# A mixture-of-experts tail: one more expert's last wide slot and remainder share a pair of tiles, and the short slots change places

## The chip, the core and the metric

The kernel runs on one core of a Trainium2 chip. The metric is device time in microseconds of one execution; what is compared is the median of several executions of each kernel. One further execution was taken by the hardware profiler; its rows are what the prediction reads.

## The reference, cut to what matters

```python
# attention, 8 batches of 2496 tokens, 256 features, z has 64
scores = (1 / S) * z @ z.T
out = u * ((maximum(scores, 0) ** 2) @ v)          # x: 19968 tokens of 256

# mixture of 8 experts, one per token
e_idx = argmax(x @ w_gate, axis=1)
for e in range(8):
    mask = e_idx == e
    h = maximum(x[mask] @ w1[e], 0)                # 256 -> 1024
    out[mask] = gate_w * sigmoid(...) * (h @ w2[e]) # 1024 -> 256
```

With the inputs of this case the experts get 2334, 2603, 2530, 2412, 2622, 1984, 2769 and 2714 tokens. Modulo 512 that leaves remainders of 286, 43, 482, 364, 62, 448, 209 and 154.

## The kernel before, in words

The first half of the time is attention. While it runs, each finished chunk of tokens is gated and scattered by GpSimd (POOL) into a list in DRAM, `xs`, that is sorted by expert. The second half, which starts near 1312 us of the span, is the mixture: a fixed list of *slots*, each with a fixed number of places n for tokens of one expert. What a slot's expert and first row are comes from small tables that the kernel computes while it runs (`full_table`, `rest_table`), so the list's shape is the same whatever the counts are.

One slot does this, in an order written out by hand in `run`:

- SyncE (SP) loads the tokens (`load_x`) and the expert's weights, 8 tiles of 256 KB (`load_w`). A slot issues these for the slot two further on. A weight load that has no `always` is skipped when the same buffers hold that expert already.
- ScalarE (ACT) and VectorE (DVE) split each weight tile into a high and a low part (`split_w`, L842 and L843), one tile at a time between the steps of the slot before; they also turn and split the next slot's tokens (`turn`, `split_x`).
- `up`: TensorE (PE) computes 1024 hidden features, 6 matmuls of n columns for each 128 of them (L897), 48 in all. The bank in PSUM is then read by ACT, which writes `hh` (L906), and by DVE, which writes `hl` (L907).
- `down`: PE multiplies back to 256 features. There are two ways. *By columns* (L976): 48 matmuls of n columns; then DVE turns the result (L986), multiplies it by the token's factor (L989), and POOL writes it out with one indirect DMA for every 32 tokens (L993), so 16 of them for 512 places and 10 for 320. *By rows* (L936): 24 matmuls of 256 columns for every 128 tokens; ACT applies the factor (L944) and POOL writes with one indirect DMA for every 128 tokens (L950). Slots of 128, 256 and 384 places go by rows, the others by columns.

The slots: 27 wide ones of 512 places (three of them by rows), and then the list that the change is about. There each expert's remainder gets a slot, and the experts are ranked by the size of the remainder. In the kernel before, the six largest have a slot of their own of 512, 448, 384, 320, 256 and 256 places, and the two smallest (62 and 43 here) are taken together with their expert's last whole 512 in a *pair* of slots that share one set of weights: 320 + 320 and 320 + 256 places. Six wide slots are left beside them. In the text the wide ones are W0 to W5, the remainders R512, R448, R384, R320, R256 and R256b, and the pairs P1a + P1b (320 + 320) and P2a + P2b (320 + 256). The order is

```
W0 R512 W1 R448 W2 R384 W3 R320 W4 R256 W5 P1a P1b P2a P2b R256b
```

The four wide ones W2 to W5 belong to one expert; W3, W4 and W5 skip their weight load. A second list (`more_slots`) behind a branch takes what does not fit; it has nothing to do with these inputs.

Of the kernel before, what the change touches and what calls it, by code (L numbers as in the profile page):

```python
# [7 lines left out]
F32 = mybir.dt.float32  # L8
F32R = mybir.dt.float32r
BF16 = mybir.dt.bfloat16  # L10
I32 = mybir.dt.int32
# [6 lines left out]
P = 128  # L18
B, S, D, DQ = 8, 2496, 256, 64
N = B * S  # L20
E, F = 8, 1024
# [3 lines left out]
TW = 512  # L25
# [2 lines left out]

N_FIRST = -(-(N - S - E * (TW - 1)) // TW)
N_MAX = N // TW - N_FIRST  # L30
N_FULL = N_MAX - E // 2 - 2

SIZES = (512, 448, 384, 320, 256, 256)

PAIRS = ((320, 320), (320, 256))

RESTS = tuple((k, 0, n) for k, n in enumerate(SIZES))
RESTS += tuple((k, at, n) for k, ab in enumerate(PAIRS, len(SIZES)) for at, n in zip((0, ab[0]), ab))
BEYOND = ((1, 384, 128), (2, 384, 128), (3, 256, 256), (4, 256, 256), (5, 256, 256), (6, 640, 384), (7, 576, 448))
ROOM = SIZES + tuple(sum(ab) for ab in PAIRS)  # L40
LENGTHS = (N_FIRST, N_MAX, E)

# [8 lines left out]
NB = CH // 32  # L51
# [9 lines left out]
def attention_moe(ctx, tc, zt, zq_in, ut, v, wg, w12, out):  # L61
# [5 lines left out]
    pool = ctx.enter_context(tc.tile_pool(name="pool", bufs=1))  # L67
# [275 lines left out]
    class Tail:  # L343
# [40 lines left out]
        def turn(self):  # L384

            w = self.w
            lt = pool.tile([P, NB, 2, 2 * E], F32, name="lt", bufs=1)
            if w < CH:
                nc.vector.memset(lt[:, w // 32 :], 0.0)
            nc.vector.transpose(out=lt.rearrange("p n k i -> p (n k i)")[:, :w], in_=self.lp[:, :w])  # L390
            self.lt = lt
# [144 lines left out]
    def t1(name, shape, dt=F32, tag=None):  # L536
        return pool.tile([1] + shape, dt, name=name, tag=tag or name)
# [146 lines left out]
    def rest_table():  # L684
# [24 lines left out]
        nc.vector.scalar_tensor_tensor(  # L709
            out=mixed, in0=rank_e, scalar=len(SIZES) - 0.5, in1=ns, op0=ALU.is_gt, op1=ALU.min  # L710
        )
# [29 lines left out]
        yield  # L741
        tab = t1("tab2", [3, len(RESTS + BEYOND)], I32)
        n = len(SIZES)
        nc.vector.tensor_copy(out=tab[:, 0, 0:n], in_=row[:, 0:n])
        nc.vector.tensor_copy(out=tab[:, 1, 0:n], in_=ex_v[:, 0:n])
        nc.vector.tensor_tensor(out=tab[:, 2, 0:n], in0=ex_v[:, 0:n], in1=ex_f[:, 0:n], op=ALU.not_equal)
        for i, (k, at, _) in enumerate((RESTS + BEYOND)[n:], n):
            if i % 4 == 0:
# [27 lines left out]
        nc.vector.tensor_scalar(  # L776
            out=over[:, E:], in0=tabs["full"], scalar1=-float(N_FULL), scalar2=None, op0=ALU.add
        )
# [8 lines left out]
    class Slot:  # L787
# [58 lines left out]
        def turn(self):  # L846
            n = self.n
            self.xf = pool.tile([P, 2, CH], F32, name="xf", tag="t", bufs=3)
            nc.vector.transpose(
                out=self.xf[:, :, 0:n].rearrange("p k (n s) -> p k n s", s=32),  # L850
                in_=self.x[:, 0 : n // 32, 0 : D // 4].rearrange("p n (k s) -> p k n s", k=2),
            )
            if self.by_rows:
                return

            self.f = pool.tile([P, NB], F32, name="fac", bufs=3)
            nc.scalar.copy(out=self.f[:, 0 : n // 32], in_=self.x[:, 0 : n // 32, SEG - 2])
            self.at = pool.tile([P, NB], I32, name="to", bufs=3)
            nc.vector.scalar_tensor_tensor(
                out=self.at[:, 0 : n // 32],  # L860
                in0=self.x.bitcast(I32)[:, 0 : n // 32, SEG - 1],
                scalar=4.0,
                in1=quarter[:, 0 : n // 32],
                op0=ALU.mult,
                op1=ALU.add,
            )
# [135 lines left out]
                tc.add_to_no_dep_group("output", it.ins)  # L1002

    kinds = [(0, i, TW, i < 3, i < 2) for i in range(N_FIRST)]
    for k in range(N_FULL):
        kinds += [(1, k, TW), (2, k, SIZES[k])]

    kinds[-1:] = [(2, i, RESTS[i][2], False, True) for i in (6, 7, 8, 9, 5)]
    more_kinds = [(1, k, TW, False, True) for k in range(N_FULL, N_MAX)]
    more_kinds += [(2, i, n, False, True) for i, (_, _, n) in enumerate(BEYOND, len(RESTS))]  # L1010
    slots, more_slots = [], []
    for part, kind in [(slots, it) for it in kinds] + [(more_slots, it) for it in more_kinds]:
        second = kind[0] == 2 and kind[1] in (7, 9)
        part.append(Slot(len(slots + more_slots), *kind, like=part[-1] if second else None))
    for part in (slots, more_slots):
        for g, s in enumerate(s for s in part if not s.like):
# [228 lines left out]
```

## Time and profile before

| | |
|---|---|
| median of 3 executions | 2601.4 us (2593.04 to 2604.06) |
| the profiled execution, its own time | 2608.31 us |
| its span, first to last instruction | 2606.3 us |
| granted TensorE clock, mean of the span | 0.93 |
| PE, DVE, ACT, POOL busy | 89%, 69%, 52%, 53% |

The shares are averages over two halves with different limits. In the first 20 of the 40 slices of the span PE is busy nine tenths or more; in the second half it is not, and only that half holds what the change touches.

### The profile page before, as it was taken

To read this page: it belongs to the slowest core of one execution; us is meant where nothing else is said; L and a number is where in the kernel's file an instruction comes from. 1 tells how busy PE (TensorE), PEld (TensorE's weight loads), DVE (VectorE), ACT (ScalarE), POOL (GpSimd) and SP (SyncE) were. 2 spreads that over 40 slices of the span, in tenths; PEclk is the share of its full clock that TensorE was granted. 3 is DMA by queue.
4 is the path that set the end of the run, shared out by engine and by line. 5 is a ranking of instruction groups with operands and counts; after the bars stand their busy time and mean duration, and the time that the engine had idled before them with its cause. 6 is when DMAs were issued, how large, how long until landed. Compare 5 with 4: busy or idle time off the path is not lost.

```text
span 2606.3 us, 34551 instructions
## 1 busy us (share of the span) xinstructions
PE 2312.5 (89%) x10266; PEld 1889.5 (72%) x10266; DVE 1795.7 (69%) x2976; ACT 1355.8 (52%) x2136; POOL 1373.0 (53%) x1234
## 2 busy tenths in 40 slices
PE   9999999999999999999977867877777777788687
PEld 7888888888888888888766645655565555577476
DVE  8988999889998899989855544444444444455343
ACT  7777677776777767777533323323333333333232
POOL 3465665656656566565543544544444444454443
PEclk9999999999999999999988988988888888898788
DMA  6776958669487695876932041221212123232220
GB/s 204 219 191 199 250 169 229 189 197 255 166 227 191 203 250 167 226 193 193 241 82 72 26 148 33 66 69 30 65 33 62 37 53 97 63 83 63 71 83 18
DMA packets 412088, 352.67 MB, mean 135 GB/s; under 512 B 127197, under 2 KB 329956, under 8 KB 411889
## 3 DMA queue, kind: packets, MB, share of 16 engines
q1 hardware_dynamic: 373168, 308.74, 43.8%
q0 software_dynamic: 38576, 41.61, 5.0%
q8 instruction: 82, 1.34, 0.2%
q14 instruction: 118, 0.96, 0.1%
q10 hardware_dynamic: 144, 0.02, 0.0%
HBM read 261.85 MB, written 139.00 MB: 154 GB/s over the span
## 4 chain that ended last, share of the span: by engine, by line
PE 46%; issue 31%; POOL 16%; DVE 3%; ACT 2%; DMA 1%; another core or an unknown queue 1%; POOLq 0%; SPq 0%; DVEq 0%; ACTq 0%
PE o L328 36%; POOL out L993 15%; PE sc L221 3%; PE sc L222 3%; PE mp L381 1%; PE o L936 1%; PE sc L897 1%; DVE al L232 1%; DVE t L244 1%; ACT a L223 1%; POOL out L950 0%; ACT a L226 0%; POOL xs L505 0%; DVE al L313 0%
## 5 line engine op out<-in xcount | busy, mean ns | idle before, releaser
L505 POOL DMA_INDIRECT xs<-xr,idx x624 | 776.5, 1244 | 545.1 <-DVE idx L501 355.4
L328 PE MATMUL o<-ah,v 128*128 128x512 f32 (+1 forms) x3200 | 967.9, 386 | 0.1
L993 POOL DMA_INDIRECT out<-y,to x550 | 549.5, 999 | 593.7 <-DVE y L989 433.8
L328 PEld LDWEIGHTS o<-ah,v 128*128 128x128 f32 x3200 | 597.2, 188 | 106.1 <-issue 0.8
L906 ACT ACTIVATE hh<-sc 128x512 fp32r<-128x512 f32 (+3 forms) x332 | 191.9, 580 | 822.1 <-remote 408.6
L328 PE MATMUL o<-al,v 128*128 128x512 f32 (+1 forms) x1520 | 589.5, 388 | 3.2 <-DVE al L232 2.0
L976 PE MATMUL o<-hh,w 128*128 128x512 f32 (+2 forms) x1152 | 410.6, 427 | 183.7 <-issue 122.1
L907 DVE SCALAR_TENSOR_TENSOR hl<-sc,hh 128x512 fp32r<-128x512 f32 (+3 forms) x332 | 220.6, 666 | 442.5 <-issue 268.7
L976 PEld LDWEIGHTS o<-hh,w 128*128 128x128 f32 x1152 | 243.1, 213 | 256.4 <-issue 141.5
L897 PE MATMUL sc<-xh,w 128*128 128x512 f32 (+4 forms) x1376 | 371.8, 385 | 64.1 <-issue 41.1
L897 PEld LDWEIGHTS sc<-xh,w 128*128 128x128 f32 x1376 | 256.5, 194 | 120.5 <-issue 49.6
L328 PEld LDWEIGHTS o<-al,v 128*128 128x128 f32 x1520 | 285.6, 188 | 68.5 <-DVE al L232 8.5
L232 DVE TENSOR_TENSOR al<-a,ah 128x1024 fp32r<-128x1024 f32 (+1 forms) x200 | 238.1, 1191 | 75.9 <-ACT ah L228 66.7
L223 ACT ACTIVATE a<-sc 128x512 f32<-128x512 f32 (+1 forms) x416 | 216.7, 572 | 109.0 <-PE sc L222 54.2
L976 PE MATMUL o<-hl,w 128*128 128x512 f32 (+2 forms) x576 | 251.7, 437 | 5.5 <-issue 5.0
L843 DVE TENSOR_TENSOR w<-raw,w 128x512 fp32r<-128x512 f32 x328 | 219.2, 680 | 21.5 <-ACT w L842 21.4
L309 ACT CAST ah<-z 128x1024 fp32r<-128x1024 f32 x192 | 199.4, 1049 | 39.6 <-DMA z<-td 31.2
L226 ACT ACTIVATE a<-a 128x1024 f32<-128x1024 f32 (+1 forms) x208 | 212.3, 1021 | 6.6
L897 PE MATMUL sc<-xl,w 128*128 128x512 f32 (+4 forms) x688 | 207.4, 383 | 2.2 <-issue 2.1
L313 DVE TENSOR_TENSOR al<-z,ah 128x1024 fp32r<-128x1024 f32 x160 | 194.7, 1217 | 13.1 <-ACT ah L309 5.9
L842 ACT CAST w<-raw 128x512 fp32r<-128x512 f32 x328 | 193.6, 615 | 0.0
L986 DVE STREAM_TRANSPOSE y<-o 128x512 f32<-128x512 f32 (+2 forms) x72 | 49.7, 691 | 168.2 <-PE o L976 136.9
(170 smaller groups left out, 2577.6 us busy)
## 6 DMA issues: line engine op xcount, KB each, us to landing
raw<-in_w SPq DMA_DIRECT2D x328, 256.0 KB
td<-t SPq DMA_DIRECT2D x160, 512.0 KB
z<-td SPq DMA_DIRECT2D x640, 128.0 KB
raw<-in_v SPq DMA_DIRECT2D x72, 256.0 KB
sx<-xs SPq DMA_DIRECT2D x136, 132.0 KB
u<-in_ut SPq DMA_DIRECT2D x32, 512.0 KB
raw<-in_zt SPq DMA_DIRECT2D x40, 256.0 KB
raw<-in_zq SPq DMA_DIRECT2D x39, 256.0 KB
```

The source lines that it names most:

```text
L223: nc.scalar.activation(out=a[:, q, :w], in_=sc[:, :w], func=AF.Relu)
L226: nc.scalar.activation(out=a[:, :, :w], in_=a[:, :, :w], func=AF.Square)
L232: nc.vector.tensor_tensor(out=al[:, :, :w], in0=a[:, :, :w], in1=ah[:, :, :w].bitcast(F32), op=ALU.subtract)
L309: nc.scalar.copy(out=ah, in_=z)
L313: nc.vector.tensor_tensor(out=al, in0=z, in1=ah.bitcast(F32), op=ALU.subtract)
L328: nc.tensor.matmul(out=o[d][:, :w], lhsT=vv[:, q, dd], rhs=rhs, start=begins and q == 0 and k == 0, stop=ends and q == 1 and k == len(term ...
L505: it = nc.gpsimd.indirect_dma_start(out=xs[:, :], out_offset=bass.IndirectOffsetOnAxis(ap=idx[:, n : n + 1], axis=0), in_=self.xr[:, n, :] ...
L843: nc.vector.tensor_tensor(out=ww[:, 1], in0=wr, in1=ww[:, 0].bitcast(F32), op=ALU.subtract)
L897: nc.tensor.matmul(out=hp[:, at : at + n], lhsT=wb[2 * d + f // 4][:, ww, fs], rhs=xx[:, d, :], start=k == 0, stop=k == 5,)
L907: nc.vector.scalar_tensor_tensor(out=lo[:, 0:w], in0=hp[:, 0:w], scalar=0.0, in1=ho[:, 0:w].bitcast(F32), op0=ALU.max, op1=ALU.subtract,)
L976: nc.tensor.matmul(out=yp[:, 0:n], lhsT=wb[4 + f // 2][:, ww, ds_], rhs=hx[:, at : at + n], start=k == 0, stop=k == 23,)
L993: it = nc.gpsimd.indirect_dma_start(out=out_quarters[:, :], out_offset=bass.IndirectOffsetOnAxis(ap=self.at[:, q : q + 1], axis=0), in_=y[ ...
```

## The change

A third expert's last whole slot and remainder become a pair, of 384 + 320 places (P0a + P0b). With it one wide slot goes (W5) and so does the second slot of 256. The list keeps 16 slots, with 6400 places where it had 6464; 13 sets of weights are loaded and split where there were 14 to split, of which three loads were skipped. All remainders and the wide slots W3 and W4 now load always. The order is

```
W0 R512 W1 R448 W2 W3 W4 R384 R256 R320 P0a P0b P1a P1b P2a P2b
```

Two small tiles (`fac`, `to`) get four buffers instead of three. The overflow list gets entries that fit the new sizes.

```diff
-N_FULL = N_MAX - E // 2 - 2
+N_FULL = N_MAX - E // 2 - 3
-SIZES = (512, 448, 384, 320, 256, 256)
-PAIRS = ((320, 320), (320, 256))
+SIZES = (512, 448, 384, 320, 256)
+PAIRS = ((384, 320), (320, 320), (320, 256))
...
-            self.f = pool.tile([P, NB], F32, name="fac", bufs=3)
+            self.f = pool.tile([P, NB], F32, name="fac", bufs=4)
-            self.at = pool.tile([P, NB], I32, name="to", bufs=3)
+            self.at = pool.tile([P, NB], I32, name="to", bufs=4)
...
-    for k in range(N_FULL):
-        kinds += [(1, k, TW), (2, k, SIZES[k])]
-
-    kinds[-1:] = [(2, i, RESTS[i][2], False, True) for i in (6, 7, 8, 9, 5)]
+    rest = [(2, i, n, False, True) for i, (_, _, n) in enumerate(RESTS)]
+    whole = [(1, k, TW, False, k > 2) for k in range(N_FULL)]
+    kinds += [whole[0], rest[0], whole[1], rest[1], *whole[2:], rest[2], rest[4], rest[3], *rest[len(SIZES) :]]
...
-        second = kind[0] == 2 and kind[1] in (7, 9)
+        second = kind[0] == 2 and kind[1] < len(RESTS) and RESTS[kind[1]][1] > 0
```

## Rows read from the trace of the kernel before

**Rows 1.** The page, part 2: busy tenths and TensorE's clock in 40 slices

```profile
PE   9999999999999999999977867877777777788687
PEclk9999999999999999999988988988888888898788
```

**Rows 2.** The page, part 4: shares of the chain that ended last

```profile
PE 46%; issue 31%; POOL 16%; DVE 3%; ACT 2%; DMA 1%; another core or an unknown queue 1%; POOLq 0%; SPq 0%; DVEq 0%; ACTq 0%
```

**Rows 3.** Waits from 2186 us: engine line, waited for, total, times, longest

```profile
POOL out L993 <- DVE y L989: 144.4, 11, 23.4
ACT hh L906 <- remote: 113.9, 23, 15.9
```

**Rows 4.** Busy time by stretch; one stretch is one slot from its first up matmul

```profile
core 0: us, PE busy (x) PEld busy (x) DVE busy (x) ACT busy (x) POOL busy (x), PEclk, DMA share, GB/s
1438.30:2285.40 847.10, 660.68 (x2498) 502.89 (x2497) 403.20 (x622) 258.44 (x470) 413.88 (x418) 0.86 0.24 61
...
2340.00:2372.30 32.30, 21.90 (x121) 20.32 (x120) 11.75 (x18) 8.47 (x17) 17.64 (x18) 0.74 0.17 42
2372.30:2394.10 21.80, 21.80 (x98) 18.04 (x97) 14.38 (x23) 11.62 (x22) 0.97 (x1) 1.00 0.42 116
2394.10:2408.30 14.20, 14.20 (x98) 14.09 (x97) 11.10 (x19) 7.55 (x16) 9.30 (x9) 1.00 0.28 55
2408.30:2452.00 43.70, 28.68 (x97) 21.38 (x97) 15.71 (x25) 10.21 (x19) 18.03 (x18) 0.73 0.25 70
2452.00:2478.90 26.90, 14.03 (x98) 12.40 (x96) 6.59 (x10) 4.51 (x9) 16.34 (x17) 0.81 0.21 61
2478.90:2502.50 23.60, 23.56 (x97) 18.95 (x98) 16.54 (x26) 12.46 (x24) 1.24 (x2) 0.93 0.58 169
2502.50:2518.20 15.70, 14.59 (x98) 14.11 (x97) 9.50 (x17) 6.17 (x14) 10.31 (x10) 1.00 0.16 37
2518.20:2548.50 30.30, 21.82 (x97) 18.74 (x97) 9.85 (x19) 6.06 (x14) 15.57 (x16) 0.72 0.11 29
2548.50:2562.60 14.10, 14.10 (x98) 14.10 (x97) 9.21 (x17) 5.91 (x13) 9.05 (x9) 1.00 0.05 18
2562.60:2586.50 23.90, 16.11 (x99) 14.05 (x98) 6.02 (x9) 3.89 (x7) 12.99 (x13) 0.79 0.06 21
2586.50:2598.20 11.70, 11.67 (x98) 11.47 (x96) 4.57 (x7) 4.79 (x9) 1.95 (x2) 1.00 0.07 23
2598.20:2606.30 8.10, 0.00 (x0) 0.00 (x0) 0.00 (x0) 0.47 (x1) 0.97 (x1) 0.71 0.04 11
```

**Rows 5.** The same view: R384's up alone, and everything behind W2

```profile
2340.00:2348.40 8.40, 8.40 (x50) 8.40 (x49) 6.91 (x11) 3.58 (x8) 4.78 (x5) 1.00 0.41 80
2340.00:2606.30 266.30, 202.46 (x1081) 177.67 (x1079) 115.20 (x188) 82.11 (x164) 114.38 (x113) 0.84 0.22 60
```

**Rows 6.** Line 993 from 1438.3 to 2285.4 us: its instructions

```profile
L993 POOL DMA_INDIRECT out<-y,to x416: 969/974/2042, 1440.8 to 2275.4; - x139
```

**Rows 7.** Timeline of POOL in R384: first and last write of W2's result

```profile
2342.40 0.97 POOL L993 DMA_INDIRECT out<-y,to  x1 [11.40 <-DVE y L989]
...
2361.70 0.97 POOL L993 DMA_INDIRECT out<-y,to  x1 [0.30 <-issue]
```

**Rows 8.** Timeline of ACT in R384: the last three of eight banks

```profile
2351.16 0.49 ACT L906 ACTIVATE hh<-sc 128x384 fp32r<-128x384 f32 x1 [5.13 <-remote]
...
2356.89 0.49 ACT L906 ACTIVATE hh<-sc 128x384 fp32r<-128x384 f32 x1 [4.74 <-remote]
2362.51 0.49 ACT L906 ACTIVATE hh<-sc 128x384 fp32r<-128x384 f32 x1 [5.12 <-issue]
```

**Rows 9.** Timeline of POOL in P2a: first and tenth write of P1b's result

```profile
2550.39 0.97 POOL L993 DMA_INDIRECT out<-y,to  x1 [8.05 <-DVE y L989]
...
2563.71 1.47 POOL L993 DMA_INDIRECT out<-y,to  x1 [0.31 <-issue]
```

**Rows 10.** The page, part 5: the splits of weight tiles

```profile
L843 DVE TENSOR_TENSOR w<-raw,w 128x512 fp32r<-128x512 f32 x328 | 219.2, 680 | 21.5 <-ACT w L842 21.4
...
L842 ACT CAST w<-raw 128x512 fp32r<-128x512 f32 x328 | 193.6, 615 | 0.0
```

More of the change, by code (lines that the diff above doesn't have):

```diff
@@ L30 @@
 N_MAX = N // TW - N_FIRST
-N_FULL = N_MAX - E // 2 - 2
-SIZES = (512, 448, 384, 320, 256, 256)
-PAIRS = ((320, 320), (320, 256))
+N_FULL = N_MAX - E // 2 - 3
+SIZES = (512, 448, 384, 320, 256)
+PAIRS = ((384, 320), (320, 320), (320, 256))
 RESTS = tuple((k, 0, n) for k, n in enumerate(SIZES))
 RESTS += tuple((k, at, n) for k, ab in enumerate(PAIRS, len(SIZES)) for at, n in zip((0, ab[0]), ab))
-BEYOND = ((1, 384, 128), (2, 384, 128), (3, 256, 256), (4, 256, 256), (5, 256, 256), (6, 640, 384), (7, 576, 448))
+BEYOND = ((1, 384, 128), (2, 384, 128), (3, 256, 256), (4, 256, 256), (5, 640, 384), (6, 640, 384), (7, 576, 448))
 ROOM = SIZES + tuple(sum(ab) for ab in PAIRS)
```

## The prediction

> **What bounds the kernel now.** I start with the page's slices [rows 1]: PE is at nine tenths through the attention half and at seven or eight in the mixture, where the change lies. The shares of the chain [rows 2] say what fills the rest: after PE, "issue" with 31% and POOL with 16%, no transfer. So I cut the end of the span into slots [rows 4], one stretch from a slot's first up matmul to the next slot's, and look for stretches longer than their PE time. They fall into two kinds. W3 takes 21.8 us with 21.8 of PE at clock 1.00, P2a 14.1 with 14.1, R256b 11.7 with 11.67. R384 takes 32.3 with 21.9 of PE, W4 43.7 with 28.68, P1b 30.3 with 21.82, P2b 23.9 with 16.11, and each of these has the clock at 0.72 to 0.81 and 13 us or more of POOL. The stretch from 1438.3 us holds 26 slots, each with a burst of 416 / 26 = 16 writes [rows 6], of 0.97 us each; they average 847.1 / 26 = 32.6.
>
> The waits [rows 3] name the cause as far as rows go: ACT's read of an up bank (L906) waits for "remote" 23 times, 113.9 us in all. R384 shows one case in full. Its up work is done on PE after 8.4 us, at 2348.4 [rows 5]. W2's result goes out meanwhile as 16 writes from 2342.40 to 2361.70 + 0.97 = 2362.67 [rows 7], one each 1.29 us. ACT reads the last three banks only at 2351.16, 2356.89 and 2362.51 [rows 8]: 5.7 us apart, the last one as the burst ends. PE stands, the clock falls, and the slot ends at 2372.30, 9.6 us after the burst. Why PE's signal reaches ACT late no row shows; I take it as a pattern. *A slot that meets a fresh POOL burst of a column slot lasts until the burst ends, plus its own down half.* Behind a slot by rows, which leaves two or three writes, a slot is clean: W3 behind R384, W5 behind R256, R256b behind P2b. A slot of 320 can escape, since its up half ends early in the burst: P1a took 15.7 and P2a 14.1 behind column slots. The next one then inherits a backlog: P1b 30.3, P2b 23.9.
>
> **What stays.** Up to 2340.0 (the end of W2) order and sizes are the same; the longer tables and the constant tiles are nothing I can see in a slot. From there before needs 266.3 us [rows 5], which is the sum of twelve stretches [rows 4] including the tail of 8.1. I rebuild that sum.
>
> **W3 and W4** now stand behind column wides, W2 and W3. Each meets a 16-write burst and gets the mean of the 26, 32.6 (bounds: R384's 32.3 and W4's 43.7, which had an older backlog; 21.8 if the burst did nothing). Both now load their weights. That is 2 MB each, issued on SP a slot or more ahead and waiting for raw tiles that ACT and DVE free; the next slot's token load is queued behind it on SP. In W5's stretch 169 GB/s x 23.6 us = 4.0 MB landed while PE ran 23.56 of 23.6 us [rows 4], so I add nothing; without that cover a set costs 2 MB / 169 GB/s = 12 us. The splits take 8 x 0.680 = 5.4 us of DVE and 8 x 0.615 = 4.9 us of ACT a set [rows 10]; these two sets were split before as well, the 26 slots hold the same, and their busy DVE is 403.2 / 847.1 = 48%. The set that goes saves as much off the path: nothing.
>
> **R384** stands behind W4 as it stood behind W2: 32.3. **R256** stands behind R384 now, so only three row writes precede it. Its bounds are R256b's clean 11.7 and its own 26.9 behind W4 today. I take 12.5, near the low one because W3, in that very place, was clean; 0.8 is added because R256b had no next slot to split for. **R320** stands behind a slot by rows as today; I give every slot of 320 that escapes 14.7, the mean of 14.2, 15.7 and 14.1.
>
> **P0a**, 384 by rows, meets R320's burst of 10. Undisturbed, ten writes take 9 x 1.29 + 0.97 = 12.6 us; a burst starts 2.4 us into the slot in R384 [rows 7] and 50.39 - 48.50 = 1.9 in P2a [rows 9], say 2.2. With R384's 9.6 behind the burst: 2.2 + 12.6 + 9.6 = 24.4. Bounds: clean, 8.4 of up and 72 down matmuls at 11.7 / 96 = 0.122, so 8.4 + 8.8 = 17.2; as R384, 32.3. I take the middle, by the burst, since its up half is R384's.
>
> **P0b** is behind a slot by rows: 14.7. **P1a** meets P0b's burst as P2a met P1b's and escapes: 14.7 (up to 30.3). That burst took 2565.18 - 2550.39 = 14.8 us in P2a [rows 9], so it ends 1.9 + 14.8 - 14.7 = 2.0 us into **P1b**. P1a's burst follows 0.3 later and takes 12.6; half of P2a's 14.1 is the down half, 7.1: 2.0 + 0.3 + 12.6 + 7.1 = 22.0 (bounds 14.1 as P2a, 30.3 as P1b today, whose backlog began with 16 writes). **P2a** is the one after such a slot, as it is today: 14.7 (14.1 to 30.3). **P2b** likewise keeps 23.9 (11.7 to 26.9) but is now last, and the tail of 8.1 comes behind it.
>
> Four buffers for `fac` and `to`: no wait on either is among the long ones, whose largest names y [rows 3]. Nothing.
>
> Sum: 32.6 + 32.6 + 32.3 + 12.5 + 14.7 + 24.4 + 14.7 + 14.7 + 22.0 + 14.7 + 23.9 + 8.1 = 247.2, against 266.3: 19.1 us less. By PE alone the swap is small: out go W5 and R256b, 21.8 + 11.7 = 33.5 clean, in come 17.2 + 14.2 = 31.4, so 2.1 less. The other 17 are the order: fewer long stalls, most of it W4 and R256.
>
> **A rule against the swap.** The 512-column W3 runs a matmul in 21.80 / 96 = 0.227 us, 0.443 ns a column; P2a of 320 in 14.1 / 96 = 0.147, 0.459 ns a column [rows 4]: narrow ones pay a little more for each place. The Trainium skill, "TensorE: Matmul & The Clock Gate", section "Back-to-back issue gap", says that each warm matmul costs its columns at 2.4 GHz and a fixed 2.5 ns on top, so that two slots in place of two others of more places save less than the places say. By that page the swap would be 96 x (215.8 + 109.2) = 31.2 us out and 96 x (162.5 + 135.8) = 28.6 in as an estimate, 2.6 less; the trace agrees with the direction, with 2.1. By the one or the other, the total would differ by half a microsecond.
>
> **From span to median.** The profiled execution took 2608.3 against a span of 2606.3, and the runs' median is 2601.4. The difference is taken off the median: 2601.4 - 19.1 = 2582.3; of the profile it would be 2589.2. Half a per cent, about what a measurement of this kernel tells from no change, is 13 us.
>
> **Rivals.** *Forecast*, 0.48: as summed. Its own range comes from P0a (17.2 to 32.3) and P1b (14.1 to 30.3), each about 8 either way and not tied to each other: 10 to 11, so 2572 to 2593.
>
> *The short slots are free*, 0.17: bursts of ten don't hold anyone. P0a gets 17.2 (-7.2), P1b 14.7 (-7.3), and P2b runs in 11.7, but its row writes queue on POOL behind P2a's burst: 16.7 us into the slot, then the tail less one write, 7.1, so 23.8 in place of 23.9 + 8.1 (-8.2). That is -41.8 in all, 2559.6. For it: P2a and R320's own clean rows. Against it: P2b today stands behind a burst of ten and took 23.9.
>
> *R256 is held as before*, 0.12: the loads of R256, R320 and P0 now follow each other behind short slots, and R256 takes 26.9. +14.4 leaves -4.7, 2596.7. Against it: the cover of W5's 4.0 MB; for it: a slot of 12 us has half of W5's time to land 2 MB in.
>
> *The end becomes a chain*, 0.23: before had two column slots of 320 in a row twice; now P0b, P1a, P1b, P2a are four, each with ten writes of at least 12.6 us against a slot of 14.7. If a backlog never drains, each behind another pays P1b's 30.3: P1a +15.6, P1b +8.3, P2a +15.6. From 19.1 on the gain is gone. Two of them, about +23.9, give 2606.2 (0.12); all three, +39.5, give 2621.8, slower than before (0.11). For it: P1b today; against it: P2a directly behind P1b ran clean, and 12.6 is less than 14.7.
>
> **Range and chances.** The predicted time is the forecast's, 2582. To leave out two in ten I reach to 2558, which takes in the free case, and to 2608, which takes in the held R256 and the chain by two, and leaves out the full chain and the outer parts of the others. Faster by over 0.5%: the free case, the forecast but for its slow edge (2588.4 and up, 0.03 of the 0.48), 0.17 + 0.45 = 0.62. Same: that edge, R256 held, and chain by two, 0.03 + 0.12 + 0.12 = 0.27. Slower: the full chain, 0.11.
>
> **What would show it.** In the changed kernel's stretches: W3 and W4 at 32 to 33 with the last L906 at the burst's end; R256 near 12 with POOL almost idle; P0a at 24 with its last bank at the end of ten writes; P1a and P2a near 14.5, P1b near 22, P2b near 24 and a tail of 8. L993 should have 544 writes for 550, L950 22 for 21, and the splits 320 for 328. The prediction is wrong if a bank's read comes late without a burst, if W3 or W4 wait for a weight tile (SP or a queue in place of "remote"), if R256 is over 20, or if a slot of 320 behind one of 320 takes 30 again.

## The result, and the profile after

The changed kernel takes 2575.2 us (the median of five executions, 2567.97 to 2586.17) where the kernel before takes 2601.4 (the median of five here as well, from 2593.04 to 2604.06): a ratio of 0.9898, 95% interval 0.9867 to 0.9929, so 26.2 us less. Forecast were 19.1 less, 2582, with a range of 2558 to 2608. In a second comparison, run with the experiments below, the ratio was 0.9943 (0.9908 to 0.9977; 2589.65 for 2604.49), 15 us less.

The profiled execution took 2586.17 us with a span of 2584.5. The slices and the chain's shares of the changed kernel, and the waits of its last slots:

```profile
PE   9999999999999999999977877787777787888797
PEclk9999999999999999999998988888888888898899
issue 45%; POOL 24%; PE 21%; DVE 4%; ACT 2%; DMA 2%; SPq 1%; another core or an unknown queue 1%; POOLq 0%; DVEq 0%; ACTq 0%
```

```profile
POOL out L993 <- DVE y L989: 128.0, 12, 15.5
ACT hh L906 <- remote: 85.3, 20, 6.4
ACT hh L906 <- PE sc L897: 144.1, 61, 10.7
```

and of the kernel before, beside [rows 3], the same engine and line with PE as the releaser:

```profile
ACT hh L906 <- PE sc L897: 113.5, 60, 9.0
```

The second half still stands at seven tenths or so, as in [rows 1]. ACT's wait for "remote" (a release that the profile can put down to no engine of this core) in the last slots fell from 113.9 us to 85.3, its longest from 15.9 to 6.4 [rows 3]. That is no gain by itself: the waits of the same line that are put down to PE rose from 113.5 to 144.1, so that both together stand at 229 where they stood at 227. The chain's shares don't bear a reading either: in the second profile of this kernel, below, PE has 47% of the chain and POOL 9%. The counts are those forecast: 544 column writes, 22 writes by rows, 320 splits.

```profile
L993 POOL DMA_INDIRECT out<-y,to x544 | 538.9, 991 | 587.7 <-DVE y L989 430.8 <-issue 156.9
L843 DVE TENSOR_TENSOR w<-raw,w 128x512 fp32r<-128x512 f32 x320 | 214.5, 680 | 20.0 <-ACT w L842 11.0 <-ACT y L944 6.7 <-DMA raw<-in_w 2.2
L950 POOL DMA_INDIRECT out<-y,meta x22 | 21.9, 995 | 74.2 <-ACT y L944 70.8 <-ACT ex L417 1.9 <-issue 1.5
```

Busy time by stretch, one slot each from the end of W2 on, in the new order W3, W4, R384, R256, R320, P0a, P0b, P1a, P1b, P2a, P2b, then the tail, then the whole; the columns are those of [rows 4]:

```profile
2349.40:2382.20 32.80, 26.50 (x97) 19.71 (x96) 15.31 (x22) 9.91 (x18) 16.05 (x16) 0.84 0.31 89
2382.20:2413.70 31.50, 24.71 (x98) 19.17 (x98) 15.93 (x23) 10.64 (x19) 15.80 (x16) 0.89 0.33 94
2413.70:2446.60 32.90, 21.97 (x122) 20.17 (x121) 10.71 (x17) 7.93 (x16) 17.53 (x18) 0.79 0.31 85
2446.60:2458.10 11.50, 11.50 (x99) 11.50 (x98) 7.58 (x13) 7.11 (x14) 1.94 (x2) 1.00 0.62 166
2458.10:2473.70 15.60, 14.84 (x99) 14.10 (x98) 12.56 (x23) 10.03 (x21) 0.97 (x1) 1.00 0.79 231
2473.70:2494.40 20.70, 18.97 (x122) 18.57 (x122) 9.87 (x17) 7.62 (x16) 11.98 (x12) 0.92 0.20 56
2494.40:2508.50 14.10, 14.10 (x99) 14.10 (x98) 8.22 (x16) 6.68 (x15) 0.97 (x1) 1.00 0.16 36
2508.50:2522.50 14.00, 14.00 (x97) 14.00 (x97) 9.55 (x18) 6.14 (x14) 9.60 (x9) 1.00 0.17 40
2522.50:2541.50 19.00, 15.61 (x98) 14.22 (x97) 8.04 (x16) 6.00 (x14) 10.69 (x11) 1.00 0.06 20
2541.50:2559.40 17.90, 15.16 (x99) 14.37 (x98) 8.02 (x16) 4.01 (x9) 9.76 (x10) 1.00 0.05 16
2559.40:2575.90 16.50, 12.86 (x97) 11.84 (x95) 4.11 (x6) 2.69 (x5) 9.71 (x10) 1.00 0.06 22
2575.90:2584.50 8.60, 0.00 (x0) 0.00 (x0) 0.00 (x0) 0.54 (x2) 1.95 (x2) 0.55 0.10 34
2349.40:2584.50 235.10, 190.21 (x1105) 171.74 (x1103) 109.91 (x185) 79.29 (x162) 106.96 (x108) 0.91 0.27 75
```

Read the two ends of the table first. Behind W2 the changed kernel needs 235.1 us where the one before needed 266.3 [rows 5]. But W2 ends at 2349.4 here and at 2340.0 there, though up to that point the two lists do the same work: single executions differ by several microseconds in the wide slots before the change even begins. So 31.2 us come from the stretch, 9.4 are lost ahead of it, and the medians say 26 and 15.

Second, the kinds of slot are those of before. W3, W4 and R384 have the clock at 0.79 to 0.89 and 15.8 us or more of POOL. R256, P0b and P1a have PE busy for the whole slot at clock 1.00. The stall of R384 is seen again in the timelines of POOL (first and sixteenth write of W4's result) and of ACT (the last three banks):

```profile
2416.14 0.97 POOL L993 DMA_INDIRECT out<-y,to  x1 [11.07 <-DVE y L989]
...
2435.32 0.97 POOL L993 DMA_INDIRECT out<-y,to  x1 [0.30 <-issue]
```

```profile
2424.79 0.49 ACT L906 ACTIVATE hh<-sc 128x384 fp32r<-128x384 f32 x1 [3.82 <-remote]
2430.58 0.49 ACT L906 ACTIVATE hh<-sc 128x384 fp32r<-128x384 f32 x1 [4.79 <-remote]
2436.89 0.49 ACT L906 ACTIVATE hh<-sc 128x384 fp32r<-128x384 f32 x1 [5.82 <-remote]
```

The burst ends at 2435.32 + 0.97 = 2436.29, the last bank is read 0.6 us later. That is the picture of [rows 7, 8].

### The profile page after: what moved, and what is told of

Read it like the earlier page. It is cut to its first block, busy times and chain, and to the rows that moved or that the text cites. A ratio compares the mean times of both kernels' runs of the same rounds, so it can differ in the third digit from the quotient of the medians.

```text
span 2584.5 us, 34512 instructions
## 1 busy us (share of the span) xinstructions
PE 2307.2 (89%) x10290; PEld 1888.0 (73%) x10290; DVE 1790.2 (69%) x2977; ACT 1352.6 (52%) x2133; POOL 1366.0 (53%) x1229
## 4 chain that ended last, share of the span: by engine, by line
issue 45%; POOL 24%; PE 21%; DVE 4%; ACT 2%; DMA 2%; SPq 1%; another core or an unknown queue 1%; POOLq 0%; DVEq 0%; ACTq 0%
PE o L328 16%; POOL out L993 15%; POOL xs L505 8%; PE sc L221 1%; PE sc L222 1%; PE o L936 1%; PE sc L897 1%; DVE al L232 1%; DVE t L244 1%; DMA z<-td 1%; PE mp L381 1%; POOL out L950 1%; DVE al L313 1%; ACT a L226 0%
## 5 line engine op out<-in xcount | busy, mean ns | idle before, releaser
L993 POOL DMA_INDIRECT out<-y,to x544 | 538.9, 991 | 587.7 <-DVE y L989 430.8
L906 ACT ACTIVATE hh<-sc 128x512 fp32r<-128x512 f32 (+3 forms) x336 | 192.0, 573 | 814.5 <-PE sc L897 394.5
L976 PE MATMUL o<-hh,w 128*128 128x512 f32 (+2 forms) x1152 | 418.3, 433 | 194.2 <-issue 122.2
L897 PE MATMUL sc<-xh,w 128*128 128x512 f32 (+4 forms) x1376 | 362.2, 378 | 42.8 <-issue 29.5
L842 ACT CAST w<-raw 128x512 fp32r<-128x512 f32 x320 | 189.1, 614 | 0.0
L976 PEld LDWEIGHTS o<-hl,w 128*128 128x128 f32 x576 | 123.7, 215 | 59.4 <-issue 28.1
```

The lines of the kernel that those rows point to most:

```text
L897: nc.tensor.matmul(out=hp[:, at : at + n], lhsT=wb[2 * d + f // 4][:, ww, fs], rhs=xx[:, d, :], start=k == 0, stop=k == 5,)
L976: nc.tensor.matmul(out=yp[:, 0:n], lhsT=wb[4 + f // 2][:, ww, ds_], rhs=hx[:, at : at + n], start=k == 0, stop=k == 23,)
L993: it = nc.gpsimd.indirect_dma_start(out=out_quarters[:, :], out_offset=bass.IndirectOffsetOnAxis(ap=self.at[:, q : q + 1], axis=0), in_=y[ ...
```

## The experiments

The theory is that of the prediction: a slot behind one by columns waits until POOL's burst of writes is over, and the change pays by which slots stand in such a place. Against it stand: the work that goes with the writes (DVE's turning and multiplying, a POOL that is merely busy), the weight loads, and a gain that comes from fewer places or from one set of weights less. The runs came from three chips (one occasion each), on which the kernel before took 2528 us (the first run of the order, the swap, half the writes, the first rows), 2604 (both kernels again, the second run of the order, all wide slots by rows) and 2613 (the rest); each ratio is to runs of before on the same chip.

**The order alone, twice.** The old sizes and pairs:

```diff
-    for k in range(N_FULL):
-        kinds += [(1, k, TW), (2, k, SIZES[k])]
-    kinds[-1:] = [(2, i, RESTS[i][2], False, True) for i in (6, 7, 8, 9, 5)]
+    rest = [(2, i, n, False, True) for i, (_, _, n) in enumerate(RESTS)]
+    whole = [(1, k, TW, False, k > 2) for k in range(N_FULL)]
+    kinds += [whole[0], rest[0], whole[1], rest[1], *whole[2:], *[rest[i] for i in (2, 4, 3, 5, 6, 7, 8, 9)]]
```

> The old sizes and pairs in the new order: W3, W4, W5 behind W2, then R384, R256, R320, the four of the pairs, R256b last. The theory (a slot lasts until the POOL burst of the column slot ahead of it ends, plus its down half) gives, with the times of the changed kernel: W3, W4, W5 and R384 32.6 each, R256 11.5, the four slots of 320 in a row 15.6, 14.1, 19.0 and 17.8, P2b 17, R256b 11.7, tail 8.1: 245 us behind W2 for 266.3 before, so 21 us less, a ratio near 0.992. If the swap of slots is what pays, this run shows no change.

Measured: 0.9981 (0.9952 to 1.001), no change that can be told. The list in this run put R256b ahead of the pairs, not last as the expectation says, so the order was run again with (2, 4, 3, 6, 7, 8, 9, 5):

> The old sizes and pairs in the new order, now with R256b at the very end (in the earlier run of the order it stood ahead of the pairs). Burst theory: W3, W4, W5, R384 30 to 33 each, R256 11.5, then R320, P1a, P1b, P2a in a row 15.6, 14.1, 19 and 18, P2b 17 to 23, R256b 11.7, tail 8: 240 to 248 us behind W2, against 235 of the changed kernel and 266 of before in the first profiles. If the order alone pays, the ratio is that of the changed kernel; by the earlier order run it is 0.998.

Measured: 0.9981 (0.9949 to 1.0013), the same. An order worth 17 us would be 0.9935, which lies outside both intervals. The stretches of the second run, W3, W4, W5, R384, R256, and the whole behind W2:

```profile
2354.40:2389.10 34.70, 26.06 (x98) 19.60 (x97) 15.30 (x22) 9.92 (x18) 15.55 (x16) 0.80 0.32 88
2389.10:2423.50 34.40, 25.77 (x98) 19.38 (x97) 15.31 (x22) 9.91 (x18) 15.54 (x16) 0.85 0.29 85
2423.50:2454.60 31.10, 24.38 (x97) 18.89 (x96) 15.92 (x23) 10.64 (x19) 15.74 (x16) 0.89 0.32 96
2454.60:2486.20 31.60, 22.64 (x122) 20.97 (x121) 10.62 (x17) 7.93 (x16) 17.50 (x18) 0.78 0.31 90
2486.20:2497.70 11.50, 11.50 (x99) 11.50 (x97) 7.56 (x13) 7.12 (x14) 1.94 (x2) 1.00 0.56 155
...
2354.40:2608.50 254.10, 198.11 (x1081) 174.06 (x1079) 116.00 (x189) 82.79 (x165) 112.47 (x113) 0.87 0.27 78
```

**The kernel before and the changed one again,** beside it on the same chip:

> The kernel before, unchanged, for its profile on the same chip as the experiments. If the chips differ only in the length of the stalls behind a burst, the clean slots (W3, R320) take 21.8 and 14.2 again, and the difference to 266.3 us behind W2 lies in R384, W4, R256, P1b and P2b.

> The changed kernel once more, beside the parts of the change. If its gain holds from chip to chip, the ratio to before is 0.990 again and the slots behind W2 take 235 us. If the gain hangs on how long the bursts hold a slot on a given chip (the earlier experiments ran on one where the kernel before took 2528 us for 2601), it is smaller where the stalls are shorter.

Of before, the stretches R384, W3, R320, W4, R256, W5, and the whole behind W2; of the changed kernel, the whole behind W2:

```profile
2337.30:2371.40 34.10, 20.71 (x121) 19.21 (x120) 11.74 (x18) 8.46 (x17) 17.61 (x18) 0.75 0.20 50
2371.40:2393.20 21.80, 21.80 (x99) 18.03 (x98) 14.38 (x23) 11.61 (x22) 0.97 (x1) 1.00 0.39 116
2393.20:2408.00 14.80, 14.69 (x98) 14.16 (x97) 10.54 (x17) 7.54 (x16) 9.68 (x9) 1.00 0.27 55
2408.00:2441.60 33.60, 28.43 (x97) 19.49 (x96) 16.11 (x26) 10.22 (x19) 16.55 (x17) 0.85 0.29 85
2441.60:2468.50 26.90, 16.01 (x97) 14.31 (x96) 6.53 (x10) 4.45 (x9) 16.33 (x17) 0.77 0.23 68
2468.50:2492.70 24.20, 24.15 (x96) 19.37 (x97) 16.59 (x26) 12.51 (x24) 1.29 (x2) 0.91 0.55 166
...
2337.30:2595.10 257.80, 202.08 (x1081) 175.44 (x1079) 115.28 (x188) 82.09 (x164) 113.32 (x113) 0.86 0.22 63
```

```profile
2348.50:2584.20 235.70, 193.76 (x1105) 175.85 (x1104) 110.57 (x185) 79.38 (x162) 107.04 (x108) 0.90 0.26 77
```

Now the order can be read, one profile each: 257.8 before, 254.1 with the order alone, 235.7 with the order and the swap. The medians of the same occasion are 2604.5, 2598.4 and 2589.7, so the swap on top of the order is 18 us by the profiles and 9 by the medians. R256 does get clean, 26.9 to 11.5, as forecast. But W3 and W5, which stood behind slots by rows and were almost clean at 21.8 and 24.2, now stand behind column slots: the wide slots and R384 take 34.7 + 34.4 + 31.1 + 31.6 = 131.8 for 34.1 + 21.8 + 33.6 + 24.2 = 113.7. That gives back 18 of what the rest gains. W4's 43.7 in the first profile [rows 4] was 33.6 here, 10.1 less, which is more than the whole difference between 266.3 and 257.8: the first profile of before had one unusually long stall.

**The swap alone,** the new sizes and pairs in the old order (with it the loads of W3 and W4 go back to the old condition):

```diff
-    whole = [(1, k, TW, False, k > 2) for k in range(N_FULL)]
-    kinds += [whole[0], rest[0], whole[1], rest[1], *whole[2:], rest[2], rest[4], rest[3], *rest[len(SIZES) :]]
+    whole = [(1, k, TW) for k in range(N_FULL)]
+    kinds += [it for k in range(N_FULL) for it in (whole[k], rest[k])] + rest[len(SIZES) :]
```

> The new sizes and pairs in the old order, wide and short in turn (W2 R384 W3 R320 W4 R256), then P0a to P2b. By the burst theory the five slots behind W2 keep their 32.3, 21.8, 14.2, 43.7 and 26.9; P0a now stands behind a slot by rows and takes its clean 17.2; then 14.1, 14.1, 19.0, 17.8 and 25.1 with the tail as in the changed kernel: 246 us, 20 us less, a ratio near 0.992. Were the swap worth only its PE time, it would be 2 us less, which cannot be told from none; were the order worth nothing, it would be the whole 26.

Measured: 0.9952 (0.9925 to 0.9979), 12 us less where 20 were expected; 242.8 behind W2 where 246 were worked out, on the chip where before was fastest and without a profile of before beside it. R256 and P0a, however, took 16.6 and 29.2 for 26.9 and 17.2:

```profile
2386.80:2403.40 16.60, 11.94 (x97) 11.59 (x95) 6.09 (x9) 4.12 (x8) 10.92 (x11) 1.00 0.30 86
2403.40:2432.60 29.20, 21.68 (x121) 20.09 (x122) 12.22 (x21) 10.33 (x22) 9.43 (x9) 0.77 0.26 80
```

Together 45.8 for 44.1. W4's burst lasted until 2410.3 us, 6.9 us into P0a, and ACT's last read of R256's result came at 2413.53, 10 us after R256's matmuls ended. So here the stall fell on the next slot: a short slot can hand a burst on.

**Half the writes.** From W2 on, every second column write is left out:

```diff
-            for q in range(nb):
+            for q in range(0, nb, 2 if self.g >= N_FIRST + 4 else 1):
```

> The changed kernel with every second write of a column slot's result left out from W2 on (half of those rows of the output are not written; all else is computed). The burst theory: a burst of 8 ends 2.4 + 10.0 = 12.4 us into the next slot, so W3, W4 and R384 take about 22 in place of 31 to 33; a burst of 5 is over before the up half of a short slot, so P0a takes 17.2 in place of 20.7, P1b and P2a 14.1 in place of 19.0 and 17.8, P2b about 12 and the tail 8: about 47 us less than the changed kernel, a ratio to before near 0.972. If what delays the slots is the work of DVE on the result (turn, multiply) or the loads, and not the writes, the times stay as in the changed kernel, 0.990.

Measured: 0.9764 (0.972 to 0.9807). W3, R384, P0a, P1b, and the whole behind W2:

```profile
2258.00:2280.00 22.00, 22.00 (x97) 17.94 (x96) 15.21 (x22) 9.82 (x18) 7.78 (x8) 1.00 0.43 130
...
2301.80:2325.20 23.40, 20.54 (x121) 19.64 (x120) 10.62 (x17) 7.93 (x16) 9.92 (x10) 0.85 0.39 112
2352.40:2369.30 16.90, 16.90 (x121) 16.90 (x120) 9.64 (x17) 7.62 (x16) 7.11 (x7) 1.00 0.22 63
2397.50:2411.60 14.10, 14.10 (x99) 14.10 (x98) 9.50 (x18) 6.21 (x14) 5.14 (x5) 1.00 0.04 13
...
2258.00:2451.60 193.60, 175.70 (x1105) 166.11 (x1103) 109.70 (x185) 79.57 (x162) 59.12 (x59) 0.96 0.29 85
```

DVE's work (15.21 us in W3) and ACT's are those of the changed kernel; only POOL's writes are halved. W3, P0a and P1b have PE busy throughout, and R384 takes 23.4 for 32.9, where a clean one takes 17. The work on DVE falls as a cause. One miss: P2b with the tail took 26.0, where about 20 was expected.

**POOL busy, but no writes.** From W2 on each column write is replaced by a fill of the result's tile:

```diff
             for q in range(nb):
+                if self.g >= N_FIRST + 4:
+                    nc.gpsimd.memset(yt, 0.0)
+                    continue
                 it = nc.gpsimd.indirect_dma_start(
```

> The changed kernel in which, from W2 on, POOL fills the result's tile with zeros 16 (10) times, about 1.1 us each, in place of each indirect write of a column slot (those rows of the output are not written). POOL is busy as long as in a burst but issues no DMA. If the writes themselves (their DMAs) hold the next slot, W3 and W4 are clean at 21.8, P0a 17.0, P1b and P2a 14.1. If a busy POOL is enough (a port or memory shared with DVE and ACT), they stay at 31 to 33, 20 and 18 to 20.

One execution. POOL's fills in W3 (one line for all sixteen), and the stretches W3, W4, R384 and the whole behind W2:

```profile
2344.57 16.17 POOL L994 MEMSET y<- 128x1024 f32 x16 [10.65 <-DVE y L989]
```

```profile
2342.20:2364.00 21.80, 21.80 (x97) 18.04 (x97) 15.21 (x22) 9.95 (x18) 15.31 (x16) 1.00 0.37 110
2364.00:2385.80 21.80, 21.80 (x98) 18.04 (x97) 15.85 (x23) 10.66 (x19) 15.31 (x16) 1.00 0.39 112
2385.80:2402.80 17.00, 17.00 (x122) 17.00 (x121) 10.37 (x17) 7.96 (x16) 13.85 (x15) 1.00 0.44 118
...
2342.20:2524.50 182.30, 171.84 (x1105) 163.39 (x1104) 109.60 (x185) 79.82 (x162) 104.01 (x108) 0.99 0.28 80
```

POOL is busy for 15.31 us of W3, against 16.05 in the changed kernel, in the same place of the slot, and the slot is clean. Behind W2 POOL is busy for 104.01 us, against 106.96, and the whole takes 182.3 for 235.1. ACT's waits ahead of L906 behind W2 come to 79.3 us for PE and none for "remote"; in the changed kernel they are 78.7 and 45.3. So it is the writes, not a busy POOL. The Trainium skill, "DMA: Bandwidth & Descriptors", section "SWDGE vs HWDGE vs iDMA", says that the descriptors of a transfer issued from GpSimd are computed in software on that engine. Whether it is this or the small transfers themselves that make ACT's reads late, no run here separates.

**The wide slots by rows,** first those of the last 16 slots, then all of them. A slot of 512 then writes the same bytes with four writes in place of sixteen:

```diff
-            self.by_rows = by_rows or n in (P, 2 * P, 3 * P)
+            self.by_rows = by_rows or n in (P, 2 * P, 3 * P) or g >= N_FIRST and n == 4 * P
```

> The changed kernel with the slots of 512 among the last 16 (W0, R512, W1, W2, W3, W4) taken by rows: 48 up matmuls of 512 and 96 down matmuls of 256 columns, four writes of 128 tokens in place of 16. By PE alone a slot costs 22.65 (slots 0 and 2, by rows already) in place of 21.8, 0.85 more each. The burst theory: R512, W1, W3, W4 go from 31 to 33 to 22.7 and R384 from 32.9 to 17.2, W0 and W2 stay held by the column slot ahead of them: about 54 us less than the changed kernel, a ratio to before near 0.97. If the bursts are not the cause, it is some 5 us more than the changed kernel, 0.992.

Measured: 0.9732 (0.9691 to 0.9773). In its profile R512, W1, W3 and W4 took 22.4 us each and R384 16.95, while W0 and W2, which still stand behind column slots, took 37.1 and 33.9: clean and held slots side by side in one execution. With `n % P == 0` in place of that condition:

> The changed kernel with every slot of 512 places by rows. Burst theory: the 23 wide slots from 1437 us to W0, which took 760.8 us in the profile of the changed kernel, take 22.65 each, 521 us, so 240 less, and the last six give some 54 as before: near 2280 us where the changed kernel takes 2575, a ratio to before of about 0.885. If POOL's bursts are not what holds the wide slots all through the mixture (or if the rows' own work on ACT and the buffers shared with the hidden layer hold them instead), each slot costs 0.85 more than now and the ratio is 0.99 to 1.00.

Measured: 0.8776 (0.8726 to 0.8825), 2283.5 us. The 24 slots from 1438.9 us in one row, and the whole behind W2:

```profile
1438.90:1977.00 538.10, 538.10 (x3459) 492.65 (x3458) 311.58 (x485) 280.55 (x504) 93.78 (x98) 1.00 0.34 88
...
2076.20:2282.10 205.90, 180.52 (x1202) 172.09 (x1200) 103.13 (x177) 84.04 (x171) 68.83 (x69) 0.96 0.29 87
```

538.1 / 24 = 22.42 a slot, PE busy throughout and clock 1.00, for 32.6 [rows 4]. The down half by rows has 96 matmuls for 48 and costs PE a little more (22.4 us a slot for 21.8), and the slot is still 10 us shorter.

**The kernel before with its wide slots by rows,** `n % P == 0` in the old list:

> The kernel before with every slot of 512 by rows, so the bursts of 16 are gone and only 448 and 320 still burst. If the change pays by what the bursts of the wide slots do (a slot of 512 in the list costs 31 to 34 behind another, and its burst holds the next), then with them gone it has next to nothing left: by PE 2 us, and the three slots of 320 in a row here against four there let this one end sooner. I work out 198 us behind W2 against 206 in the changed kernel by rows: 2275 for 2283, equal within 10. If the change pays for another reason (fewer places, one set of weights less to split), this kernel is 15 to 26 us slower than the changed one by rows, 2298 to 2310.

Measured: 0.8732 (0.8686 to 0.8777), 2279.5 us; the changed list by rows had 0.8776, on another of the chips. The whole behind W2:

```profile
2070.90:2276.60 205.70, 182.07 (x1226) 173.67 (x1224) 106.32 (x175) 88.25 (x175) 62.63 (x62) 0.95 0.28 78
```

205.7 here, 205.9 there: without the bursts of the wide slots the change is worth nothing that can be told. I had worked out 198 here, 8 too few.

**The loads of W3 and W4** under the old condition, which skips both:

```diff
-    whole = [(1, k, TW, False, k > 2) for k in range(N_FULL)]
+    whole = [(1, k, TW) for k in range(N_FULL)]
```

> The changed kernel with the weight loads of W3 and W4 under the old condition, by which both are skipped (they then compute with other experts' weights). 4 MB less are loaded. If the added loads are hidden, as the prediction has it, W2, W3 and W4 keep their 30 to 36 us each and the stretch behind W2 its 235; if they hold a slot, up to 12 us a set come off.

Measured, in one execution: 233.2 us behind W2 for 235.1 and 235.7, W3 and W4 at 33.1 and 33.5 for 30 to 35, with 4.2 MB less loaded. Nothing of the 12 us a set shows; the loads are hidden, but for the 2 us or so that one profile can't tell.

**Every slot by rows,** those of 448 and 320 too, which end in a block of 64 tokens:

```diff
-            for q in range(self.n // P):
-                y = ys[:, q]
+            for q in range(-(-self.n // P)):
+                c = min(P, self.n - q * P)
+                y = ys[0:c, q]
...
-                    ts = slice(at + q * P, at + (q + 1) * P)
+                    ts = slice(at + q * P, at + q * P + c)
```

> The changed kernel with every slot by rows, those of 448 and 320 places too (a last block of 64 tokens). Against the run with only the wide slots by rows: R448 is to cost 9.7 + 96 x 0.122 = 21.4 for 19.5 and each slot of 320 7.1 + 72 x 0.122 = 15.9 for 14.1 clean; but W2 goes from 34.9 to 22.4, P0a from 21.0 to 17.0, P1b and P2a from 18.7 and 17.9 to 15.9, P2b with the tail from 31.3 to about 20: some 27 us less than that run's 2283, so 2257, a ratio to before near 0.867. If ten writes behind a slot of 320 hold nobody, the dearer down halves make it some 8 us slower than that run.

Measured: 2257.8 us, 0.8644 (0.8586 to 0.8702). Behind W2:

```profile
2064.40:2256.10 191.70, 180.29 (x1322) 175.63 (x1320) 94.61 (x157) 90.63 (x181) 33.23 (x35) 0.98 0.32 94
```

This version takes 13.6% less than the kernel before; the changed kernel takes 0.6 to 1.0% less. The short bursts cost as well: it is 14.2 us shorter behind W2 than the run with only the wide slots by rows, though each slot of 320 has a dearer down half (15.5 us for 14.1 clean).

## Why the prediction was right, and where it was not

The forecast's terms, in us, against the first profile and the second of the changed kernel:

| slot | forecast | first | second |
|---|---|---|---|
| W3, W4 | 32.6 + 32.6 | 32.8 + 31.5 | 35.0 + 30.1 |
| R384 | 32.3 | 32.9 | 31.6 |
| R256 | 12.5 | 11.5 | 11.5 |
| R320 | 14.7 | 15.6 | 15.6 |
| P0a | 24.4 | 20.7 | 20.1 |
| P0b, P1a | 14.7 + 14.7 | 14.1 + 14.0 | 14.1 + 14.1 |
| P1b, P2a | 22.0 + 14.7 | 19.0 + 17.9 | 20.2 + 18.6 |
| P2b and tail | 32.0 | 25.1 | 24.9 |
| sum | 247.2 | 235.1 | 235.7 |

- **The pattern** held for the slots behind 16 writes, and its cause is now shown and not only read: half the writes make the slot 22.0, writes replaced by fills make it 21.8, four writes in place of sixteen make it 22.4. Why ACT's reads come late behind such writes stays open.
- **W3, W4, R384, R256 and the loads** came as summed, within 2.5 us each.
- **P0a** was sized as if its own 9.6 us followed the burst. R320's burst of ten ended at 2488.3, and the slot at 2494.4, 6.1 later: ACT read the last bank 2.7 us ahead of the burst's end. 20.7 for 24.4. Behind ten writes a slot is held for less than the pattern says.
- **The end** was mis-sized. The three slots P1b, P2a, P2b and the tail were put at 68.7 and took 62.0 and 63.7. P1b, P2a and P2b each took a small delay (at clock 1.00 in the first profile, at 0.84 to 0.92 in the second), in place of one clean slot between two long ones. That is 7 of the 12 us by which the sum was too high. What decides between the two ways is not shown: in the second run of the order, where four slots of 320 stand in a row too, P1b, P2a and P2b took 23.3, 14.1 and 23.8, as forecast. One difference between that list and the changed one is a term that the prediction put at nothing, the fourth buffer of `fac` and `to`. No wait on either tile shows in the profiles of the two kernels, but the buffers were never run by themselves, so they are not ruled out.
- **The base** hid most of that on the other side. The sum was set against 266.3, a profile with a stall of 43.7 in W4; the second profile of before has 257.8. The stretch so fell by 31 in one pair of profiles and by 22 in the other; 26 and 15 are the medians. That 19.1 lies between those is in part luck: two errors, 12 in the sum and 8.5 in the base, went against each other.
- **The step that failed** is the split of the gain: "By PE alone the swap is small" and "The other 17 are the order". The order alone gave 0.998, twice, about 5 us, and 3.7 us in the profile; the swap alone gave 0.9952, 12 us, and on top of the order 254.1 - 235.7 = 18.4 us by the profiles and 9 by the medians. Both forecast halves lie outside the measured intervals; which half is worth more they don't settle, as the intervals of the two runs overlap. The swap was priced by clean times, 33.5 out and 31.4 in. But in the new order a wide slot costs 30 to 35, not 21.8: the wide slots and R384 together fell by 35.1 (131.8 to 96.7), what stands behind P1a fell by 17.5, R256b's 11.7 among it, and P0a and P0b came in with 34.2. And the order pays back what it wins: it frees R256 and spoils the two clean places of W3 and W5. The two halves had to be priced one on top of the other, in the places they end up in.
- **A sum in the rule against the swap** takes P0a for 96 matmuls of 384 columns. By rows it has 48 of 384 and 72 of 256, which makes the estimate 28.7 us in for 28.6; nothing hangs on it.
- **The rivals.** The free case is refuted as a rule: P0a and P1b are held. In the sum, though, the run lies about midway, with 235.1 us behind W2 between the forecast's 247.2 and the free case's 266.3 - 41.8 = 224.5, and P2b with its tail came close to what the free case gave it, 25.1 for 23.8. R256 isn't held as before. The chain doesn't build up. The lists without the wide slots' bursts show what the change is worth for its own sake: nothing that can be told.

## What to carry to other kernels

When a slot is slow, look at what the slot ahead of it leaves running, and price a slot by the place it will stand in, not by its own clean time. Before the order of such slots is tuned, try to remove what they hand on: here a down half with twice the matmuls and a quarter of the writes was worth over ten times the change of order and sizes. Compare single stretches only across several profiles: one long stall in one of them was 10 us, where the whole effect is 15 to 26.

## What the runs showed of the hardware

While POOL issues a run of indirect writes, one each 1.29 us, ACT reads banks that PE has finished late: in the 26 slots from 1438.3 us of the kernel before, the wait ahead of L906 was put down to "remote" 65 times, 321.8 us in all, 5.0 in the mean. In those slots ACT stood idle only ahead of L906; its splits (L842), which need nothing of PE, never waited. That points at PE's signal and not at ACT, but it is a reading and no run tests it. Behind ten writes the delay was smaller: P0a's last three banks in the first profile of the changed kernel were read 2.2 and 2.8 us apart. Fills of the same length on POOL hold up nothing (W3 at 21.8). Nor is it the bytes: 512 x 256 values in four writes leave the next slot at 22.4 us, in sixteen at 30 to 35.

How much it holds differs from chip to chip, or from occasion to occasion, which these runs don't separate: W0 starts at 2120 to 2137 us in the four profiles of the first experiments' chip and at 2186 to 2198 in the other seven with the wide slots by columns ahead of it. The 23 wide slots ahead of W0 took 747.1 us in a profile of the one kind (the kernel before) and 699.7 in one of the other (the swap alone), 32.5 and 30.4 a slot, while clean slots took the same to 0.1 us on both (21.8 for 512 by columns, 14.1 for 320).

```profile
1439.00:2186.10 747.10, 582.02 (x2209) 442.91 (x2208) 356.40 (x554) 227.77 (x414) 363.45 (x370) 0.87 0.23 60
```

```profile
1437.40:2137.10 699.70, 577.02 (x2209) 444.25 (x2208) 356.33 (x559) 227.56 (x414) 366.86 (x370) 0.88 0.24 64
```
